# Gate sums scattered as sums and inverted on gathered rows, a count on GpSimd, and splits of expert 0's weights at other places

## The chip, the cores and the metric

The kernel runs on one core of a Trainium2 chip. The metric is device microseconds of one execution, start to end. The core's engines are TensorE (PE), VectorE (DVE), ScalarE (ACT) and GpSimd (POOL); SyncE (SP) issues the loads.

## What is computed

A linear attention with decay (4 batches, 8 heads, 768 tokens, head size 48), then a mixture of 8 experts in which each of the 3072 tokens goes to its best expert alone:

```python
for t in range(S):
    cur = np.einsum('bhd,bhe->bhde', u[None] * kt, vt)
    y[:, :, t] = np.einsum('bhd,bhde->bhe', rt, state + cur)
    state = wt[:, :, :, None] * state + np.einsum('bhd,bhe->bhde', kt, vt)
...
logits = x @ w_gate                       # x: 3072 x 384, w_gate: 384 x 8
expert_idx = np.argmax(logits, axis=1)
logits_shift = logits - logits.max(-1, keepdims=True)
probs = np.exp(logits_shift)
probs /= probs.sum(-1, keepdims=True) + 1e-09
gate_w = probs[np.arange(N), expert_idx]
for e in range(E):
    mask = expert_idx == e
    h = np.maximum(x[mask] @ w1[e], 0.0)  # w1[e]: 384 x 1024
    ye = h @ w2[e]                        # w2[e]: 1024 x 384
    out[mask] = gate_w[mask, None] * ye
```

The chosen expert's shifted logit is 0 and its exponential 1, so a token's weight is 1 over the sum of its 8 exponentials (and 1e-9).

## The kernel before

**The token loop.** Tokens are worked in blocks of 128 (a chunk) of one batch: NB = 24 blocks, 6 chunks of B = 4 batches. `iteration(n)` runs for n = -3 to 23 and holds work of several blocks at once. For a block, DVE runs two scans over decays (`suf` and `pre`), the products `kh` and `rh`, and `at`, which puts the masked products `ap` of PE beside the diagonal. POOL forms `rk` and clears triangles of `at` (L359); PE does the products; ACT copies diagonals (`at` L371), evicts (`ytb`, `xr`, `ls`) and scales states. `keep_warm` puts products of constants into PE's queue, whose result nobody reads: six in the coefficients of n = 0 and 1, two in some others.

**The gate.** GB = 8 blocks, a pair of chunks, go through the gate together (n = 9 and 17 for the first two pairs; the last pair goes in smaller groups). For each token DVE takes the maximum logit, the shifted logits `sh` and the one-hot `oh` of the choice. `count` adds the one-hots over the blocks (`ohs`) to the running `seen`; `place` works out each token's row in its expert's region, summing to `pf` and casting it to the integer `pi`; `act_ex` is the exponential `ex` on ACT, and `weigh` (n = 10 and 18) sums it (`se`), adds 1e-9 and writes the reciprocal into column DM of `xr`. A row of `xr` is a token's 384 values, then its weight (column DM), then its number. POOL scatters these rows to `xs` in memory by expert (an indirect DMA for each block). Rows that no token takes were filled before from `zrow`.

**The experts.** Products run in pairs of halves: each f32 weight is split into a high half (`w1h`, `w2h`, by ACT, L246) and a low one (`w1l`, `w2l`, by DVE, L248), the rows likewise (`x` and the second `x`, L301 and L302; hidden values `hh` L311 and `hl` L312), and three products stand for one. Expert 0's rows are worked in two parts of 192 and 236 rows: `pa` within the loop's end (`pa.trans`, `pa.mm1(0)` to `pa.mm1(7)`), `pb` behind it. `contract` is the second product of a part: 24 products into a bank `opt` for each half of the rows, evicted by `ort` on DVE (L325), which multiplies each row by its weight in column DM; POOL scatters `ort` to the output. Experts 1 to 7 follow in order of their token count, each with one load of rows (`load_x`, tile `xg`), a transposing split (`trans_x`), `mm1` and `mm2`.

**What sets the order.** Within the loop and the first expert the order on PE, DVE, ACT and POOL is written out by hand; behind it a scheduler sets it. SP's order is the order in which loads are written: the load of expert 1's rows stands behind the last token scatter and pb's rows, ahead of expert 1's remaining weights. Expert 0's weights are loaded early and are split in pieces of 128 x 512: twelve high halves, one for each n from 8 to 19, and the six w1 lows at n = 11, 12, 13, 14, 15 and 19, right behind `at`; the six w2 lows at n = 22 and 23 (two each, behind `at`) and two among `pa.mm1`.

## Time and profile before

| | |
|---|---|
| median of 3 runs | 408.28 us (407.12 to 409.44) |
| the profiled execution | 405.56 us |
| its span in the trace | 403.9 us |
| busy, share of the span: PE, DVE, ACT, POOL | 94%, 66%, 58%, 29% |
| instructions on PE, DVE, ACT, POOL | 3537, 493, 651, 162 |
| mean granted TensorE clock | 0.988 of full speed |

The span is what the trace covers; the profiled execution lasted 1.7 us more than it. The token loop takes the span's first 160 us or so, the experts the rest. Shares are means over both, so they are read by stretch. Line numbers L... are those of the kernel before; in the changed kernel the same lines stand 4 to 18 further down.

### The profile page before, as it was taken

To read this page: it belongs to the slowest core of one execution; us is meant where nothing else is said; L and a number is where in the kernel's file an instruction comes from. 1 tells how busy PE (TensorE), PEld (TensorE's weight loads), DVE (VectorE), ACT (ScalarE), POOL (GpSimd) and SP (SyncE) were. 2 spreads that over 40 slices of the span, in tenths; PEclk is the share of its full clock that TensorE was granted. 3 is DMA by queue.
4 is the path that set the end of the run, shared out by engine and by line. 5 is a ranking of instruction groups with operands and counts; after the bars stand their busy time and mean duration, and the time that the engine had idled before them with its cause. 6 is when DMAs were issued, how large, how long until landed. Compare 5 with 4: busy or idle time off the path is not lost.

```text
span 403.9 us, 9402 instructions
## 1 busy us (share of the span) xinstructions
PE 380.3 (94%) x3537; PEld 339.5 (84%) x3538; DVE 267.0 (66%) x493; ACT 234.0 (58%) x651; POOL 118.1 (29%) x162
## 2 busy tenths in 40 slices
PE   8898899898998889999999999999999999999994
PEld 6576677777776668989988999999999999999994
DVE  8799699999999997647774662562562672632321
ACT  8699799899999873236564543543552562420210
POOL 5543233495436946210300050040040050221001
PEclk9699999999999999999999999999999999999998
DMA  8999999999851223395789247246246244011001
GB/s 198 192 202 190 235 278 220 227 293 250 209 125 60 74 77 119 89 320 159 223 265 297 82 127 228 90 141 214 82 140 216 78 138 138 5 51 38 18 2 54
DMA packets 30159, 62.05 MB, mean 154 GB/s; under 512 B 4880, under 2 KB 17979, under 8 KB 30109
## 3 DMA queue, kind: packets, MB, share of 16 engines
q1 hardware_dynamic: 25500, 51.92, 48.7%
q0 software_dynamic: 4608, 9.48, 7.1%
q8 instruction: 29, 0.48, 0.5%
q14 instruction: 22, 0.17, 0.1%
HBM read 49.53 MB, written 12.20 MB: 153 GB/s over the span
## 4 chain that ended last, share of the span: by engine, by line
PE 65%; DVE 19%; ACT 6%; DMA 4%; issue 3%; POOL 1%; SPq 1%; POOLq 0%; ACTq 0%; DVEq 0%
PE bank L309 24%; PE bank L968 17%; PE opt L321 10%; DVE at L400 4%; DVE pre L393 4%; DVE suf L377 3%; PE ap L498 2%; PE pt L300 2%; DMA xg<-xs 2%; DVE kh L387 2%; PE op L957 2%; ACT at L371 2%; DMA rkwt<-in_rkw_dram 2%; PE lp L548 2%; PE kp L489 1%
## 5 line engine op out<-in xcount | busy, mean ns | idle before, releaser
L272 POOL DMA_INDIRECT out_dram<-ot,xg x26 | 30.1, 1159 | 169.3 <-DVE ot L958 126.8
L248 DVE TENSOR_TENSOR w2l<-wst,w2h 128x512 fp32r<-128x512 f32 x48 | 31.1, 682 | 42.5 <-ACT w2h L246 42.5
L309 PE MATMUL bank<-xl,w1h 128*128 128x384 f32 (+5 forms) x168 | 58.8, 353 | 0.0
L309 PE MATMUL bank<-xh,w1l 128*128 128x384 f32 (+5 forms) x168 | 58.4, 350 | 0.0
L309 PE MATMUL bank<-xh,w1h 128*128 128x384 f32 (+5 forms) x168 | 54.2, 355 | 0.0
L311 ACT ACTIVATE hh<-bank 128x384 fp32r<-128x384 f32 (+7 forms) x58 | 26.3, 470 | 39.0 <-PE bank L309 38.0
L371 ACT ACTIVATE at<-ident,ct 128x128 f32<-128x128 f32 x144 | 47.0, 395 | 0.0
L312 DVE SCALAR_TENSOR_TENSOR hl<-bank,hh 128x384 fp32r<-128x384 f32 (+7 forms) x58 | 29.8, 530 | 22.8 <-ACT hh L311 22.6
L344 POOL TENSOR_TENSOR rk<-rkwt 112x512 f32<-112x512 f32 x24 | 32.2, 1342 | 37.0 <-DVE pre L381 30.2
L498 PE MATMUL ap<-rh,kh 48*128 48x128 f32 (+1 forms) x384 | 29.2, 291 | 7.9 <-DVE rh L354 5.8
L248 DVE TENSOR_TENSOR w1l<-wst,w1h 128x512 fp32r<-128x512 f32 x48 | 31.4, 686 | 6.7 <-ACT w1h L246 6.0
L498 PEld LDWEIGHTS ap<-rh,kh 64*128 64x128 f32 (+1 forms) x384 | 24.3, 193 | 13.2 <-DVE rh L354 10.1
L246 ACT ACTIVATE w1h<-wst 128x512 fp32r<-128x512 f32 x48 | 28.5, 627 | 11.9 <-DMA wst<-in_w_dram 6.7
L400 DVE COPY_PREDICATED at<-cmask,ap 128x1024 f32<-128x1024 int32 x24 | 31.6, 1318 | 4.8 <-PE ap L498 4.4
L973 ACT ACTIVATE oT<-bank 128x464 f32<-128x464 f32 (+4 forms) x15 | 7.9, 523 | 46.2 <-PE bank L968 46.2
L968 PE MATMUL bank<-hh,w2l 128*128 128x408 f32 (+4 forms) x96 | 34.0, 356 | 0.0
L968 PE MATMUL bank<-hl,w2h 128*128 128x408 f32 (+4 forms) x96 | 33.9, 354 | 0.0
L968 PE MATMUL bank<-hh,w2h 128*128 128x408 f32 (+4 forms) x96 | 33.7, 356 | 0.0
L695 POOL DMA_INDIRECT xs<-xr,pi x24 | 28.8, 1198 | 16.6 <-DVE sh L569 5.4
L377 DVE TENSOR_TENSOR_SCAN suf<-rkwt,sufone 112x520 f32<-112x520 f32 x24 | 31.2, 1300 | 1.7 <-DMA rkwt<-in_rkw_dram 1.7
L309 PEld LDWEIGHTS bank<-xh,w1l 128*128 128x128 f32 x168 | 31.6, 188 | 0.8
L309 PEld LDWEIGHTS bank<-xl,w1h 128*128 128x128 f32 x168 | 31.4, 188 | 0.7
(169 smaller groups left out, 865.0 us busy)
## 6 DMA issues: line engine op xcount, KB each, us to landing
rkwt<-in_rkw_dram SPq DMA_DIRECT2D x44, 289.5 KB, 9.7
wst<-in_w_dram SPq DMA_DIRECT2D x48, 256.0 KB, 5.5
wst<-in_w_dram SPq DMA_DIRECT2D x16, 768.0 KB, 7.7
vt<-in_vv_dram SPq DMA_DIRECT2D x24, 192.0 KB, 9.0
xg<-xs SPq DMA_DIRECT2D x6, 579.0 KB, 5.4
xs<-zrow SPq DMA_DIRECT2D x8, 289.5 KB, 9.1
rkwt<-in_rkw_dram SPq DMA_DIRECT2D x4, 224.0 KB, 4.5
xg<-xs SPq DMA_DIRECT2D x1, 675.5 KB
```

The source lines that it names most:

```text
L248: nc.vector.tensor_tensor(out=lo, in0=st[:, cs], in1=hi.bitcast(F32), op=ALU.subtract)
L272: i = nc.gpsimd.indirect_dma_start(out=out[:, :], out_offset=bass.IndirectOffsetOnAxis(ap=t.bitcast(I32)[:, q, DM + 1:DM + 2], axis=0), in ...
L309: nc.tensor.matmul(hp, a, x[:, j, :], start=(i == 0), stop=(i == 8))
L312: nc.vector.scalar_tensor_tensor(out=hl, in0=hp, scalar=0.0, in1=hh.bitcast(F32), op0=ALU.max, op1=ALU.subtract)
L321: nc.tensor.matmul(op, a[:, cs], w2v(wt, w, f), start=(i == 0), stop=(i == 23))
L344: i = nc.gpsimd.tensor_tensor(out=d["rk"], in0=d["r"], in1=d["k"], op=ALU.mult)
L371: nc.scalar.activation(blk[n]["at"][:, j, q], ident, AF.Copy, scale=blk[n]["ct"][:, head(q, j):head(q, j) + 1])
L377: nc.vector.tensor_tensor_scan(out=suf[:, ::-1], data0=d["w"][:, ::-1], data1=sufone.rearrange("p q c -> p (q c)")[:, ::-1], initial=0.0, ...
L400: nc.vector.copy_predicated(out=d["at"].rearrange("p j q c -> p (j q) c"), mask=cmask.unsqueeze(1).broadcast_to([P, 2 * NP_, C]), data=d[" ...
L498: nc.tensor.matmul(d["ap"][:, j, q, :], d["kh"][rs, q, :], d["rh"][rs, q, :], start=True, stop=True)
L695: i = nc.gpsimd.indirect_dma_start(out=xsf, out_offset=bass.IndirectOffsetOnAxis(ap=ch["pi", c, b], axis=0), in_=xr[:, b, :], in_offset=No ...
L968: nc.tensor.matmul(pp, w, a, start=(i == 0), stop=(i == 23))
```

## The change

- `weigh` no longer inverts. The sums are written straight into column DM of `xr`; the 1e-9 is a ninth column of the two constant tiles `exs` that take turns for `ex`. The reciprocal is taken in place on the gathered rows: `pa.weights()`, `pb.weights()`, and at the head of `mm2` for experts 1 to 7. `zrow` gets 1.0 in column DM.
- `count` of a pair of chunks is four additions on GpSimd in place of a reduction and an addition on DVE.
- `place` sums straight to an integer; the cast is gone.
- The six high halves of w2 move from n = 14 to 19 to n = 22 and 23. The w1 lows of n = 14, 15 and 19 move to n = 22 (two) and 23 (one). All six w2 lows move behind `pa.mm1(7)`.
- `contract` does the 16 products with `w2h` first, then the 8 with `w2l`.
- `keep_warm` puts ten products at n = 1, not six.

```diff
     ebrow = const.tile([1, GB, E], BF16, name="ebrow")
     none = const.tile([1, 1], F32, name="none")
+    exs = [const.tile([P, GB, E + 1], F32, name=f"ex{i}") for i in range(2)]
     zrow = wst.tile([P, XC], F32, name="zrow", tag="wst")
...
         nc.gpsimd.memset(zrow, 0.0)
+        nc.gpsimd.memset(zrow[:, DM:DM + 1], 1.0)
...
+        for t in exs:
+            nc.gpsimd.memset(t[:, :, E:E + 1], 1e-9)
...
         op = xtile([rows, DM], "opt")
         i = 0
-        for f in range(8):
-            hh, hl = hs[f]
-            cs = slice(q * rows, (q + 1) * rows)
-            for a, w in ((hh, "h"), (hl, "h"), (hh, "l")):
-                nc.tensor.matmul(op, a[:, cs], w2v(wt, w, f), start=(i == 0), stop=(i == 23))
-                i += 1
+        cs = slice(q * rows, (q + 1) * rows)
+        for part in ("hl", "h"):
+            for f in range(8):
+                for x in part:
+                    nc.tensor.matmul(op, hs[f][x == "l"][:, cs], w2v(wt, "h" if part == "hl" else "l", f), start=(i == 0), stop=(i == 23))
+                    i += 1
...
-            keep_warm(t[:, C:], 6 if n < 2 else 2 if n < B or n - 3 in (2 * B, 4 * B) else 0)
+            keep_warm(t[:, C:], 10 if n == 1 else 6 if n < 2 else 2 if n < B or n - 3 in (2 * B, 4 * B) else 0)
...
     def act_ex(k):
-        ex = sm.tile([P, GB, E], F32, name="ex", tag="ex")[:, 0:k[2]]
-        nc.scalar.activation(ex, ch["r", k][0], AF.Exp)
+        ex = exs[nth["e"] % 2][:, 0:k[2]]
+        nth["e"] += 1
+        nc.scalar.activation(ex[:, :, 0:E], ch["r", k][0], AF.Exp)
...
         add = oh[:, 0, :]
-        if m > 1:
+        if m == GB:
+            part, w = oh, m // 2
+            while w:
+                half = sm.tile([P, w, E], F32, name="ohh", tag=f"ohh{w}", bufs=1)
+                nc.gpsimd.tensor_tensor(out=half, in0=part[:, 0:w], in1=part[:, w:2 * w], op=ALU.add)
+                part, w = half, w // 2
+            add = part[:, 0, :]
+        elif m > 1:
             add = sm.tile([P, E], F32, name="ohs", tag="ohs")
             nc.vector.tensor_reduce(out=add, in_=oh.rearrange("p b e -> p e b"), axis=AX.X, op=ALU.add)
-        nc.vector.tensor_tensor(out=new, in0=old, in1=add, op=ALU.add)
+        (nc.gpsimd if m == GB else nc.vector).tensor_tensor(out=new, in0=old, in1=add, op=ALU.add)
...
         c, b, m = k
-        se = sm.tile([P, GB], F32, name="se", tag="se")[:, 0:m]
-        nc.vector.tensor_reduce(out=se, in_=ch["ex", k], axis=AX.X, op=ALU.add)
-        nc.vector.tensor_scalar(out=se, in0=se, scalar1=1e-9, scalar2=None, op0=ALU.add)
         for i in range(0, m, B):
             w = min(B, m - i)
-            nc.vector.reciprocal(ch["xr", c + i // B][:, b:b + w, DM], se[:, i:i + w])
+            nc.vector.tensor_reduce(out=ch["xr", c + i // B][:, b:b + w, DM], in_=ch["ex", k][:, i:i + w], axis=AX.X, op=ALU.add)
...
-        pf = sm.tile([P, GB], F32, name="pf", tag="pf")[:, 0:m]
-        nc.vector.tensor_reduce(out=pf, in_=ps, axis=AX.X, op=ALU.add)
         pi = sm.tile([P, GB], I32, name="pi", tag="pi", bufs=3)[:, 0:m]
-        nc.vector.tensor_copy(pi, pf)
+        with nc.allow_low_precision("whole numbers below 2 ** 24"):
+            nc.vector.tensor_reduce(out=pi, in_=ps, axis=AX.X, op=ALU.add)
...
+        def weights(self):
+            nc.vector.reciprocal(self.t[:, :, DM:DM + 1], self.t[:, :, DM:DM + 1])
+
         def mm2(self, q):
             contract(wt0, self.hs, q, self.rows, self.t)
...
     lows = []
-    late = []
-
-    def late_lows(k):
-        for _ in range(k):
-            split_piece(*late.pop(0), half="l")
+    late = [(wt0, i, 3, p) for i in (2, 3) for p in range(3)]
+
+    def late_splits(half, ks):
+        for k in ks:
+            t, i, n, p = late[k]
+            split_piece(t, stg[0, i], i, n, p, half)
...
         dve_state(n - 1)
         dve_at(n)
-        if n in (11, 12, 13, 14, 15, 19):
+        if n in (11, 12, 13):
             split_piece(*lows.pop(0), half="l")
-        if n >= NB - 2:
-            late_lows(2)
+        for _ in range(2 if n == NB - 2 else 1 if n == NB - 1 else 0):
+            split_piece(*lows.pop(0), half="l")
         act_diag(n + 1, slice(0, 1) if n < 0 else slice(0, 3))
         if whole and b == 2:
             weigh(whole)
+        if n == NB - 2:
+            late_splits("h", range(0, 3))
...
             act_ex(pair)
+            late_splits("h", range(3, 6))
             place(pair)
...
-        m = n - 8
-        if 0 <= m < 12:
-            piece = (wt0, stg[0, m // 3], m // 3, 3, m % 3)
+        if 8 <= n < 14:
+            piece = (wt0, stg[0, (n - 8) // 3], (n - 8) // 3, 3, (n - 8) % 3)
             split_piece(*piece, half="h")
-            (lows if m < 6 else late).append(piece)
+            lows.append(piece)
...
         wt = wts[e % 2]
+        nc.vector.reciprocal(t[:, :, DM:DM + 1], t[:, :, DM:DM + 1])
...
         weigh(mid)
-        late_lows(1)
         pe_y(nl)
...
         count(end)
-        late_lows(1)
         pa.mm1(2)
...
         pa.mm1(7)
+        late_splits("l", range(6))
+        pa.weights()
         expert(1)
         pb = Part(HA, HB // 2)
         load_x(1)
...
         pb.trans()
         pa.mm2(1)
+        pb.weights()
         nth["b"] = 0
```

How this stands on the engines. First DVE from the last `hl` of `pa.mm1(7)` on, with `xg_2593` (before) and `xg_2589` (after) the gathered rows of `pa`, `xg_3026` those of `pb` and `xg` without a number those of expert 1 (`116x4`); before:

```order
L312 SCALAR_TENSOR_TENSOR hl<-bank,hh 128x192
L325 TENSOR_SCALAR ort<-opt,xg_2593 96x384
L302 TENSOR_TENSOR x_3047<-pt,x_3047 128x236 x3
L325 TENSOR_SCALAR ort<-opt,xg_2593 96x384
L312 SCALAR_TENSOR_TENSOR hhl<-bank,hhl 128x236 x2
L248 TENSOR_TENSOR w1l<-wst,w1h 128x512 x3
L312 SCALAR_TENSOR_TENSOR hl<-bank,hh 128x236 x3
L248 TENSOR_TENSOR w1l<-wst,w1h 128x512 x3
```

and after:

```order
L316 SCALAR_TENSOR_TENSOR hl<-bank,hh 128x192
L252 TENSOR_TENSOR w2l<-wst,w2h 128x512 x6
L733 RECIPROCAL xg_2589<-xg_2589 96x2
L953 RECIPROCAL xg<-xg 116x4
L329 TENSOR_SCALAR ort<-opt,xg_2589 96x384
L306 TENSOR_TENSOR x_3029<-pt,x_3029 128x236 x3
L329 TENSOR_SCALAR ort<-opt,xg_2589 96x384
L733 RECIPROCAL xg_3026<-xg_3026 118x2
L316 SCALAR_TENSOR_TENSOR hhl<-bank,hhl 128x236 x2
L252 TENSOR_TENSOR w1l<-wst,w1h 128x512 x3
L316 SCALAR_TENSOR_TENSOR hl<-bank,hh 128x236 x3
```

Six lows of w2 and two reciprocals stand between the last `hl` and the first `ort`, the second of them on expert 1's rows; that on pb's rows follows the second `ort`.

DVE at n = 9 and 10, from `place` to behind `weigh`; before:

```order
L632 TENSOR_TENSOR ps<-few,oh 128x64
L634 TENSOR_REDUCE pf<-ps 128x8
L636 CAST pi<-pf 128x8
L377 SCALAR_TENSOR_TENSOR suf<-rkwt,sufone 112x520
L381 RECIPROCAL pre_0_175<-suf 112x4
L408 TENSOR_TENSOR sst_190<-dp,gbd_189 112x192
L400 COPY_PREDICATED at<-cmask,ap 128x1024
L600 TENSOR_REDUCE se<-ex 128x8
L601 TENSOR_SCALAR se<-se 128x8
L604 RECIPROCAL xr<-se 128x4 x2
L387 TENSOR_TENSOR kh<-rkwt,suf 112x512
```

and after:

```order
L641 TENSOR_TENSOR ps<-few,oh 128x64
L644 TENSOR_REDUCE pi<-ps 128x8
L381 SCALAR_TENSOR_TENSOR suf<-rkwt,sufone 112x520
L385 RECIPROCAL pre_0_175<-suf 112x4
L412 TENSOR_TENSOR sst_190<-dp,gbd_189 112x192
L404 COPY_PREDICATED at<-cmask,ap 128x1024
L613 TENSOR_REDUCE xr<-ex_215 128x4 x2
L391 TENSOR_TENSOR kh<-rkwt,suf 112x512
```

Place is one instruction shorter; of the four of `weigh` two reductions are left.

POOL around the count of the first pair; before:

```order
L344 TENSOR_TENSOR rk<-rkwt 112x512
L359 AFFINE_SELECT at<-ct 128x256
L344 TENSOR_TENSOR rk<-rkwt 112x512
L359 AFFINE_SELECT at<-ct 128x256
L344 TENSOR_TENSOR rk<-rkwt 112x512
L607 IOTA xr 128x4
L359 AFFINE_SELECT at<-ct 128x256
L344 TENSOR_TENSOR rk<-rkwt 112x512
```

and after:

```order
L348 TENSOR_TENSOR rk<-rkwt 112x512
L363 AFFINE_SELECT at<-ct 128x256
L348 TENSOR_TENSOR rk<-rkwt 112x512
L363 AFFINE_SELECT at<-ct 128x256
L348 TENSOR_TENSOR rk<-rkwt 112x512
L599 TENSOR_TENSOR ohh<-oh 128x32
L599 TENSOR_TENSOR ohh<-ohh 128x16
L599 TENSOR_TENSOR ohh<-ohh 128x8
L605 TENSOR_TENSOR seen<-seen,ohh 128x8
L616 IOTA xr 128x4
L363 AFFINE_SELECT at<-ct 128x256
```

Four additions stand ahead of the row numbers (`IOTA xr`), where there were none.

## Rows read from the trace of the kernel before

**Rows 1.** Busy time by stretch (us, busy time with count per engine, PEclk, DMA share, GB/s).

```profile
67.00:99.00 32.00, 29.16 (x476) 22.54 (x474) 31.38 (x52) 29.57 (x100) 18.59 (x24) 1.00 1.01 254
118.00:138.00 20.00, 16.79 (x290) 13.22 (x293) 19.63 (x35) 18.21 (x63) 13.58 (x17) 1.00 0.15 53
168.00:400.00 232.00, 229.10 (x1319) 220.78 (x1317) 113.28 (x198) 93.03 (x188) 35.36 (x30) 1.00 0.44 137
```

**Rows 2.** Chain of waits in the token loop (start us, length us, engine and line).

```profile
70.79 0.17 DVE ohs L592
...
70.98 0.17 DVE seen L593
...
73.80 0.23 DVE pf L634
...
74.13 1.25 DVE suf L377
...
77.07 0.10 DVE se L600
...
77.20 0.18 DVE se L601
...
77.40 0.24 DVE xr L604 x2
...
100.82 0.57 DVE w1l L248
```

**Rows 3.** Timeline of Pool and DVE from 12.2 us (start, length, [idle before <- releaser]).

```profile
12.25 0.40 POOL L359 TENSOR_SCALAR_AFFINE_SELECT at<-ct 128x256 f32<-128x256 f32 x1
...
12.78 1.27 POOL L344 TENSOR_TENSOR rk<-rkwt 112x512 f32<-112x512 f32 x1
12.89 2.25 DVE L377 TENSOR_TENSOR_SCAN suf<-rkwt,sufone 112x520 f32<-112x520 f32 x1 [0.93 <-DMA rkwt<-in_rkw_dram]
```

**Rows 4.** Timeline of ACT in the last blocks.

```profile
149.21 0.27 ACT L551 ACTIVATE ls<-lp 64x128 f32<-64x128 f32 x1 [1.77 <-PE lp L548]
```

**Rows 5.** Groups by line: the high halves of a split (busy us, mean ns).

```profile
L246 ACT ACTIVATE w2h<-wst 128x512 fp32r<-128x512 f32 x48 | 27.8, 626 | 4.9 <-DMA wst<-in_w_dram 3.3 <-PE bank L968 1.4
```

**Rows 6.** Timeline of DVE around the first expert.

```profile
168.17 0.36 DVE L312 SCALAR_TENSOR_TENSOR hl<-bank,hh 128x192 fp32r<-128x192 f32 x1 [0.21 <-ACT hh L311]
171.99 0.61 DVE L325 TENSOR_SCALAR ort<-opt,xg 96x384 f32<-96x384 f32 x1 [3.47 <-PE opt L321]
...
180.78 1.90 DVE L248 TENSOR_TENSOR w1l<-wst,w1h 128x512 fp32r<-128x512 f32 x3 [0.28 <-ACT w1h L246]
```

**Rows 7.** Timeline of PE around the first expert.

```profile
172.66 0.42 PE L300 MATMUL pt<-ident,xg 118*128 118x118 f32 x2 [0.20 <-DVE ort L325]
173.16 0.42 PE L321 MATMUL opt<-w2h,hh 128*96 128x384 f32 x1
```

**Rows 8.** SP's waits, 165 to 180 us (us in total, times, longest).

```profile
SPq L235 <- DMA xg<-xs: 1.8, 1, 1.8
```

**Rows 9.** Timeline of SP's DMA issues, 165 to 180 us.

```profile
168.38 1.92 SPq L266 DMA_DIRECT2D xg<-xs  x4
...
175.59 0.38 SPq L235 DMA_DIRECT2D wst<-in_w_dram  x1
```

**Rows 10.** Timeline of PE and DVE at the start.

```profile
9.78 1.14 PE L143 MATMUL cp<-wz,ones 128*128 128x384 bf16 x6
...
12.35 0.66 PE L475 MATMUL cp<-rk,ubt 112*32 112x128 f32 x8 [1.43 <-POOL rk L344]
...
16.35 1.31 DVE L400 COPY_PREDICATED at<-cmask,ap 128x1024 f32<-128x1024 int32 x1 [0.99 <-PE ap L498]
```

**Rows 11.** Busy time and granted clock (PEclk) at the start.

```profile
5.35:12.18 6.83, 5.12 (x36) 2.49 (x34) 6.51 (x9) 5.23 (x11) 3.89 (x2) 1.00 1.06 223
12.18:19.00 6.82, 6.66 (x48) 4.47 (x49) 5.08 (x5) 4.66 (x17) 3.88 (x7) 0.50 1.05 182
```

More of the change, by code (lines that the diff above doesn't have):

```diff
@@ L87, in small @@
         return few["t"]
-    nth = {"b": 0, "h": 0, "x": 0}
+    nth = {"b": 0, "h": 0, "x": 0, "e": 0}
     def xtile(shape, name):
```

## Prediction

> **What bounds the kernel now.** The page's busy times, taken over the whole span, put PE first by far. That mean hides two kernels in one, so the first view to read is the busy time by stretch [rows 1]. From 168 us on, in the experts, PE is busy 229.10 of 232.00 us: there any microsecond in which PE stands is a microsecond of the result. In the token loop it is different. From 67 to 99 us DVE is busy 31.38 of 32.00 us, from 118 to 138 us 19.63 of 20.00, while PE has 29.16 and 16.79. Matching this, the chain of waits runs for long stretches from one DVE instruction into the next [rows 2]. So in the loop, work taken from DVE counts nearly in full, and after the loop only what stops or frees PE counts. The change does something to each side: it empties DVE in the loop, and it puts a wait in front of PE's work at about 172 us.
>
> **DVE work taken out of the loop.** I go by the chain's own pieces [rows 2].
> - Count of a pair (n = 9 and 17): ohs 0.17 and seen 0.17 with the 0.02 between them leave DVE: 0.36 each, 0.72 together.
> - Place (n = 9 and 17): from the start of pf (73.80) to that of suf (74.13) are 0.33. A reduce alone takes about 0.16 before the next one follows. Saved 0.17 each, 0.34 together.
> - Weigh (n = 10 and 18): from 77.07 to the end of xr are 0.57 for four instructions; two reduces of about the size of se (0.18 to 0.25 from start to start) stay. Saved about 0.22 each, 0.44 together.
> - Low halves w1l at n = 14, 15 and 19: 0.57 on the chain at 100.82, and two more pieces like it; 1.71 together.
>
> The sum is 3.21 us. The six w2h pieces leave ACT in n = 14 to 19 as well, so ACT does not take DVE's place as the bound in these blocks.
>
> **What that costs elsewhere.** Three w2h pieces come to stand before `ls` of n = 22 and three behind `ex` of n = 23. ACT waits there for PE anyway, 1.77 us before the `ls` of n = 22 [rows 4] and longer before the next, and three pieces of 0.63, as splits on ACT take [rows 5], need 1.9: nothing, or 0.1. The three w1l lows go to n = 22 and 23 and replace four w2l lows there: nothing. The count goes to Pool as four small instructions. Pool's price is bounded by its 0.40 for a 128x256 select and its 1.27 for a 112x512 product [rows 3]; four operands of 128x32 and less should take 0.2 each. Pool's own time is free at n = 9. But two engines can hold each other up: a suf that started 0.11 behind Pool's rk took 2.25 [rows 3], against 1.25 in the loop [rows 2], so it waited about as long as rk ran. A DVE instruction that meets one of the four small ones then loses up to 0.2 to 0.4. I take 0.2 per pair, at least 0 and at most 0.5. The loop's gain is thus 2.8 us, between 2.2 and 3.2.
>
> On this the Trainium skill ("SBUF — State Buffer", section "Who interferes with whom") says that a DVE instruction with two SBUF inputs and a GpSimd instruction that reads SBUF exclude each other for the whole instruction, whichever began first. The 2.25 agrees. If each of the four met such a DVE instruction, the rule would make it 0.8 per pair instead of 0.2, and the gain 1.6.
>
> **The reciprocals, and the wait that they bring.** The sums' reciprocals are now taken on the gathered rows, nine small instructions of about 0.2 us. Eight of them find their rows landed long before or sit where DVE idles. One does not. On DVE, behind the last `hl` of the first part, the new order is: six w2l lows, the reciprocal of part one's rows, **the reciprocal of expert 1's rows**, and only then `ort`, which evicts the first `opt`. Expert 1's rows are loaded late: SP issues that load with the last two of the four issues that fill 168.38 to 170.30 [rows 9], behind the last token scatter. The first thing that shows its landing is SP's wait for it before a weight load, 1.8 us long [rows 8], after which that load is issued at 175.59 [rows 9]. So the rows land at about 175.45; the small second piece of the same load, issued last, may land up to 0.7 later.
>
> Until now nothing needed these rows before PE transposes them, after both parts of the first expert are done. Now `ort` does, and behind it on DVE are the second half of pb's split (`x` minus) and the second `ort`. Who waits for that: PE. In the trace, PE stood 0.20 us on the first `ort` and began the second `opt` at 173.16 [rows 7], with `ort` running 171.99 to 172.60 [rows 6]. In the new order:
> - The six lows begin when `hl` ends (168.53) [rows 6] and take 3.8, since three such took 1.90 [rows 6]: done at 172.3. As `contract` now takes all high products first, PE meets the lows late, and the first `opt` ends some 0.5 us later than it did.
> - The last scatter begins 0.6 to 0.8 earlier relative to PE, since one cast, one TENSOR_SCALAR, one reciprocal and a low no longer stand before it; so the rows are there at 174.7 to 175.4, against PE's old time.
> - Reciprocal 0.2, `ort` 0.61, the two last transposes 0.42: the second `opt` begins between 175.9 and 177.0, not at 173.16.
>
> PE loses 3.3 us (2.6 to 3.9). A little could be won back at later short waits of PE; with PE busy 229.10 of 232.00 us [rows 1] I take nothing for it. Uncovered, this wait alone is larger than the loop's gain. SP's queue is not reordered, and Pool's scatters of `ort` have time.
>
> **The start.** Between 5.35 and 12.18 us the granted clock was 1.00 and between 12.18 and 19.00 it was 0.50 [rows 11], the lower of TensorE's two levels, 1.2 against 2.4 GHz. What came before was an idle gap of PE of 1.43 us, until Pool's rk was done, ending at 12.35 [rows 10]. Six dummy products took 1.14 [rows 10]; ten fill about 0.7 of this gap. If the clock then holds, DVE's idle 0.99 before the first `at` [rows 10] goes, and in the blocks behind it the chain runs over PE too: 0.5 to 1.6, I take 1.1. If it doesn't, the four dummies lie in a gap and cost nothing. I see no reason in the trace for one or the other: one half each.
>
> **The sum.** -2.8 (loop) + 3.3 (wait) + 0 (ACT, SP) gives +0.5 with the old start, and -0.6 with a start at full clock. The profiled execution took 405.56 us, 403.9 of them the span, 2.7 less than the median 408.28; the difference is added to the median. That is 408.8 or 407.7; I say 408.2. No measurable change, then, 0.5% (2.0 us) being about what a measurement of this kernel can tell from none.
>
> **The rivals.**
> 1. *The wait is followed by half clock* (slower). PE idle for 3.3 us in one piece is more than all of PE's idle time from 168 to 400 us, 2.90 [rows 1], and the one stretch at half clock, 6.82 us long [rows 11], followed a gap of less than half that. If PE's idle time at 173 to 176 brings such a stretch, the products behind it take twice their time: 3.4 us lost, with PE as the bound. Then 408.2 + 3.4 = 411.6 (410 to 412.5). It decides from the point at which the gap is long enough to make the clock fall; the trace has only the one case to go by. The Trainium skill ("TensorE: Matmul & The Clock Gate", section "Why this matters for your kernels") warns that an idle gap between bursts of products puts the engine back on its low clock; it speaks for this rival, and this case's one fall agrees.
> 2. *The wait isn't there* (faster). Either the load lands earlier than SP's wait tells, or the wait on the second piece falls where DVE has nothing else. For it: the landing is known from another engine's wait alone. Against: SP's queue stood 1.8 us for it, until just before 175.59 [rows 8, 9]. Then -2.8, with either start: 404.4 to 405.5.
> 3. *Pool eats the gain.* In n = 18 to 21 two token scatters per block stand in Pool's queue, and if Pool sets the pace once DVE has less, what n = 18 and 19 gave (0.22 and 0.57) is lost, and with locks at the upper bound another 0.6: 1.4 of the 2.8, 409.6. Against it: from 118 to 138 us Pool is busy 13.58 of 20.00 us [rows 1].
>
> **How the numbers follow.** Forecast, the wait with the clock kept: 0.45 (406.7 to 409.5). Rival 1: 0.31. Rival 2: 0.16. Rival 3: 0.08, on the border of measurable. Faster by over 0.5% is rival 2 and the edge of the forecast (a load that lands early, and a full-clock start): 0.18. Slower is rival 1 and part of rival 3: 0.35. The rest, 0.47, is within 0.5%. The range leaves out the faster half of rival 2 and the upper edge of rival 1: 404.7 to 411.9.
>
> **What would show it.** DVE's list at 170 to 177 must show `ort` idle before it, ended by the DMA of xg, and PE a gap of about 3 us before the second `opt`; the granted clock of the 7 us behind that gap decides rival 1. The last `hl` of the first part, at 168.17 before [rows 6], should start 2.8 us earlier, or 3.9 with the start's gain; the granted clock of 12 to 19 us tells the start. If DVE's chain is broken by waits for Pool in n = 18 to 21, rival 3 holds. The forecast is wrong if PE's gap is under 1 us, or if the loop gives less than 2.

## The result and the profile after

| | before | changed | ratio (95%) |
|---|---|---|---|
| median of 4 runs each | 407.77 us (407.12 to 409.44) | 413.33 us (412.83 to 414.86) | 1.0136 [1.0093, 1.018] |
| the profiled execution | 405.56 us | 412.84 us | |
| its span | 403.9 us | 411.1 us | |
| its mean granted clock | 0.988 | 0.972 | |

Slower by 1.4%, and outside the range of 404.7 to 411.9. But the two sides did not run at the same clock: the four changed runs had mean granted clocks of 0.964 to 0.976, the one run of before whose clock is listed 0.988. The same file was therefore timed twice more, on two chips (experiments 5 and 9): 1.0011 [0.9977, 1.0045] and 1.0013 [0.9968, 1.0059], at clocks of 0.975 to 0.996. In experiment 9 two more runs, at 0.963 and 0.962, took 414.33 and 414.96 us, which is where the four changed runs above lie. So there are two questions: what the change itself does, which is close to nothing in sum, and where the first measurement's 5.6 us came from. (The ratios leave out runs more than 1.5% above the fastest of the same measurement, so the four changed runs, all alike, stay in; the profiles of experiments 4, 11 and 12 were taken in such runs, and no time after their first 60 us is compared.)

The page of the changed kernel: busy times, and the granted clock in 40 slices of the span (9 is full).

```profile
PE 386.0 (94%) x3541; PEld 344.5 (84%) x3542; DVE 265.8 (65%) x480; ACT 234.0 (57%) x651; POOL 123.3 (30%) x173
...
PEclk9999999999999759969999999999999999999998
```

The dents stand in slices 14, 15 and 18, not at the start. The busy times by stretch tell them apart (columns as in [rows 1]: busy time per engine, then granted clock, DMA share, GB/s):

```profile
5.35:12.18 6.83, 6.38 (x49) 3.33 (x48) 6.76 (x8) 5.23 (x11) 4.57 (x3) 1.00 1.05 237
12.18:19.00 6.82, 5.49 (x72) 4.01 (x72) 6.72 (x8) 6.79 (x25) 4.29 (x7) 1.00 1.08 206
135.06:141.89 6.83, 4.80 (x55) 3.51 (x53) 5.10 (x11) 4.94 (x19) 3.53 (x8) 0.78 0.32 99
141.89:148.72 6.83, 6.46 (x62) 5.03 (x62) 3.01 (x7) 4.63 (x15) 0.30 (x1) 0.50 0.08 28
148.72:155.54 6.82, 6.74 (x69) 5.45 (x68) 2.70 (x14) 3.85 (x11) 4.28 (x8) 0.72 0.31 116
...
176.46:183.28 6.82, 5.96 (x20) 5.28 (x21) 1.74 (x5) 0.37 (x1) 0.94 (x1) 0.50 0.84 305
```

The start, at half clock before [rows 11], is now at full clock. In its place there are two other stretches at 0.50: 13.65 us at the loop's end (138.91 to 152.56) and 6.82 us from 176.46. The second lies exactly where the prediction looked. DVE's timeline around the first expert (start, length, idle before and its releaser), then PE's:

```profile
169.44 0.36 DVE L316 SCALAR_TENSOR_TENSOR hl<-bank,hh 128x192 fp32r<-128x192 f32 x1
169.72 3.69 DVE L252 TENSOR_TENSOR w2l<-wst,w2h 128x512 fp32r<-128x512 f32 x6
...
176.55 0.18 DVE L953 RECIPROCAL xg<-xg 116x4 f32<-116x4 f32 x1 [3.07 <-DMA xg<-xs]
176.65 0.61 DVE L329 TENSOR_SCALAR ort<-opt,xg 96x384 f32<-96x384 f32 x1
```

```profile
173.46 0.59 PE L325 MATMUL opt<-w2l,hh 128*96 128x384 f32 x2 [0.19 <-DVE w2l L252]
173.90 0.57 PE L304 MATMUL pt<-ident,xg 118*128 118x118 f32 x4
177.32 0.66 PE L304 MATMUL pt<-ident,xg 118*128 118x118 f32 x2 [2.86 <-DVE ort L329]
177.64 0.65 PE L325 MATMUL opt<-w2h,hh 128*96 128x384 f32 x1
178.09 0.53 PE L325 MATMUL opt<-w2h,hl 128*96 128x384 f32 x1
```

DVE, in order, stands 3.07 us on expert 1's rows with `ort` behind it; PE stands 2.86 us on `ort` [rows 7: 0.20 before]; and the products behind it start 0.32 to 0.45 us apart, where those of the first `opt` in the same profile started 0.17 to 0.18 apart.

The span split at the same instructions, changed minus before in us; 'same clock' is the profile of experiment 5, the same file, whose only half-rate stretch, apart from the last microseconds, is 3.41 us long:

| stretch | changed | same clock |
|---|---|---|
| start to `at` of n = 5 | -3.3 | -2.2 |
| to `at` of n = 21 | -2.8 | -3.6 |
| to the first `opt` product (loop's end) | +7.4 | +0.2 |
| to the first `ort` | +3.4 | +3.7 |
| to the third `ort` (behind the wait) | +2.4 | +0.9 |
| to the end | +0.2 | +1.3 |
| sum | +7.3 | +0.3 |

(The last stretch took 212.8 to 214.5 us in the profiles of all kernels but those three, 213.15 in that of before, in no order with the edits.)

### The profile page after: what moved, and what is told of

It is laid out like the page before. It is cut to its first block, busy times and chain, and to the rows that moved or that the text cites. A ratio compares the mean times of both kernels' runs of the same rounds, so it can differ in the third digit from the quotient of the medians.

```text
span 411.1 us, 9418 instructions
## 1 busy us (share of the span) xinstructions
PE 386.0 (94%) x3541; PEld 344.5 (84%) x3542; DVE 265.8 (65%) x480; ACT 234.0 (57%) x651; POOL 123.3 (30%) x173
## 4 chain that ended last, share of the span: by engine, by line
PE 64%; DMA 11%; DVE 10%; ACT 6%; POOL 4%; issue 3%; SPq 1%; POOLq 0%; ACTq 0%; DVEq 0%
PE bank L313 24%; PE bank L983 17%; PE opt L325 9%; DMA xg<-xs 3%; DMA rkwt<-in_rkw_dram 3%; PE ap L502 2%; PE pt L304 2%; DVE at L404 2%; DMA xs<-zrow 2%; DMA vt<-in_vv_dram 2%; DVE pre L397 2%; DVE suf L381 2%; PE yp L538 2%; PE op L972 2%; POOL xs L703 2%
## 5 line engine op out<-in xcount | busy, mean ns | idle before, releaser
L502 PE MATMUL ap<-rh,kh 64*128 64x128 f32 (+1 forms) x384 | 29.3, 294 | 8.3 <-DVE rh L358 7.0
L703 POOL DMA_INDIRECT xs<-xr,pi x24 | 29.8, 1241 | 19.9 <-DVE mx L571 7.2
L250 ACT ACTIVATE w2h<-wst 128x512 fp32r<-128x512 f32 x48 | 27.3, 625 | 7.5 <-DMA wst<-in_w_dram 6.0
```

The lines of the kernel that those rows point to most:

```text
L250: nc.scalar.activation(hi, st[:, cs], AF.Copy)
L502: nc.tensor.matmul(d["ap"][:, j, q, :], d["kh"][rs, q, :], d["rh"][rs, q, :], start=True, stop=True)
L703: i = nc.gpsimd.indirect_dma_start(out=xsf, out_offset=bass.IndirectOffsetOnAxis(ap=ch["pi", c, b], axis=0), in_=xr[:, b, :], in_offset=No ...
```

## The experiments

My theory after the result: the wait costs about what was predicted, the clock falls behind it each time, and the loop-end fall is either the change's own doing (PE idles more once DVE is quicker) or chance. The rival: the moved splits hold up the loop's end. 'Changed' below is the kernel after the change.

| | edit | ratio to before (95%) |
|---|---|---|
| 1, 10 | expert 1's reciprocal late | 0.9898 [0.9823, 0.9972]; 0.994 [0.9897, 0.9983] |
| 2 | dummies in the loop's end | 0.9991 [0.9929, 1.0054] |
| 3 | both of these | 0.9939 [0.9856, 1.0022] |
| 4 | before, ten dummies | 0.9916 [0.9836, 0.9997] |
| 5, 9 | changed, again | 1.0011 [0.9977, 1.0045]; 1.0013 [0.9968, 1.0059] |
| 6, 11 | 1, splits at their old places | 0.9917 [0.9883, 0.9951]; 0.9987 [0.9943, 1.0032] |
| 7 | before, with the wait alone | 1.0102 [1.0069, 1.0134] |
| 8 | changed, wait filled with dummies | 1.0043 [1.0003, 1.0083] |
| 12 | 1, w2's lows spread | 0.9937 [0.9887, 0.9986] |

Experiments 1 to 4, 5 to 8 and 9 to 12 ran on three different chips.

**1. The wait taken away.** Expert 1's reciprocal moves behind `pb.mm2(1)`, where its rows have long landed.

```diff
-        nc.vector.reciprocal(t[:, :, DM:DM + 1], t[:, :, DM:DM + 1])
+        if e > NST:
+            nc.vector.reciprocal(t[:, :, DM:DM + 1], t[:, :, DM:DM + 1])
...
         pb.mm2(1)
+        nc.vector.reciprocal(xg[1][:, :, DM:DM + 1], xg[1][:, :, DM:DM + 1])
```

> The changed kernel, but the reciprocal of expert 1's rows is taken behind the second part's last eviction, when the rows have long landed, instead of ahead of the first eviction of the first part. Theory: PE's stand of 2.86 us at 174.5 (row of the changed kernel's trace, ended by ort) goes, and with it the half-rate stretch from 176.46 to 183.28, which costs half of 6.8 us: 413.3 - 2.9 - 3.4 = 407.0, and the granted clock stays 1.00 from 160 us on. Rival, the second fall of the clock has another cause (it came 37.5 us after the first): only 2.9 goes, 410.4, with a half-rate stretch in the experts.

Faster than before. DVE's `ort` now waits only for PE, and the clock behind it stays up:

```profile
169.56 0.61 DVE L329 TENSOR_SCALAR ort<-opt,xg 96x384 f32<-96x384 f32 x1 [0.61 <-PE opt L325]
```

```profile
138.28:141.70 3.42, 3.42 (x31) 3.02 (x32) 1.11 (x6) 2.78 (x12) 0.41 (x1) 0.50 0.38 109
168.00:176.00 8.00, 7.34 (x44) 6.14 (x44) 3.36 (x9) 0.99 (x3) 0.94 (x1) 1.00 0.99 324
```

From the first `opt` product to the first `ort` it takes 5.22 us, 4.38 before and 7.77 in the changed kernel. The 0.84 that stay are the six lows in a row, which PE meets late. The loop's end has a fall here too, but of 3.42 us, not 13.65, and up to 169 us the two programs are the same.

**2. Dummies in the loop's end.** Four dummy products ahead of `ap` for n = 18 to 21 and six in the coefficients of n = 22 and 23; the reciprocal stays early.

```diff
+            keep_warm(t[:, C:], 6 if n in (22, 23) else 0)
...
+            if 18 <= n < 22:
+                keep_warm(d["ap"][:, 0, 0:3, :].rearrange("p q c -> p (q c)"), 4)
```

> The changed kernel with products of constants put into PE's queue, results unread: four ahead of ap at n = 18 to 21 and six behind the coefficients at n = 20 and 21. Theory: the half-rate stretch from 138.91 to 152.56 follows PE's gaps there (1.37 at 128.82, 1.66 at 139.16); filled, the clock holds, and the gain of 6.1 us that at shows at n = 21 (135.53 against 141.61) reaches the first expert: 413.3 less about 6.8 = 406.5. Rival, the loss between n = 21 and the first expert comes from the moved splits on ACT and DVE or from Pool's scatters and not from the clock: the dummies add up to 2 us of PE work in the last blocks, 413 to 415.

The clock held from 139 to 153 us, but the dummies stood ahead of `ap` in PE's queue: `at` of n = 21 came at 138.61, against 134.66 in experiment 1 on the same chip, and at n = 23 it was still 1.7 behind (151.96 against 150.26). They cost more than they saved. The fall behind the wait was there (174.53 to 177.95).

**3. Both.** The edits of 1 and 2 together.

```diff
+        if e > NST:
...
+            keep_warm(t[:, C:], 6 if n in (22, 23) else 0)
...
+                keep_warm(d["ap"][:, 0, 0:3, :].rearrange("p q c -> p (q c)"), 4)
```

> Both edits: the reciprocal of expert 1's rows late, and the dummy products at n = 18 to 21. Theory: both losses go, 413.3 - 6.3 - 6.8 = 400.2, with the granted clock at 1.00 throughout. Rival, moved splits and Pool set the end of the loop: about 407, as with the late reciprocal alone.

No stretch at half clock before the tail, and yet not distinguishable from 1 or from before. Even so `at` of n = 23 began 8.2 us after that of n = 22 (5.9 before), DVE idle 2.51 ahead of it: something other than the clock delays the loop's end here (see the last section).

**4. Before with ten dummies at n = 1.**

```diff
-            keep_warm(t[:, C:], 6 if n < 2 else 2 if n < B or n - 3 in (2 * B, 4 * B) else 0)
+            keep_warm(t[:, C:], 10 if n == 1 else 6 if n < 2 else 2 if n < B or n - 3 in (2 * B, 4 * B) else 0)
```

> The kernel before with ten dummy products in place of six in the coefficients of n = 1, nothing else. Theory: the changed kernel's early gain is the start's: its at was 1.30 us earlier at n = 0 and 3.31 at n = 8, before any other edit acts, and the clock was 1.00 between 12 and 19 us instead of 0.50. So 407.8 - 3.3 = 404.5 if the clock then holds to the end. Rival, the start's clock depends on where the run's phase falls and not on the dummies: 0.50 between 12 and 19 us again, 407.8.

`at` of n = 5 begins 2.9 us earlier than in the profile of before, at full clock. By itself this would give the start's gain to the dummies; experiment 7 takes it back. The ratio, 0.9916, has its interval just below 1, from three runs, and was not measured again.

**5. The changed kernel again, on another chip.** No edit.

> The changed kernel as it is, on the chip of the runs beside it. Up to 169 us it is the same program as the one with the late reciprocal, which had its clock at half for 3.4 us in the loop (138.28 to 141.70) where the changed kernel had 13.65 (138.91 to 152.56). Theory: the length of that stretch varies from chip or run, and the changed kernel is here about 6.3 above the late reciprocal's 404.9 (2.9 of waiting, 3.4 of half clock behind it): 411. Rival: the loop's long half-rate stretch belongs to the changed kernel in every run: 413, as at first.

404.63 against 404.54 us. Profile: windows as above, of the loop's end and of the 3.41 us behind the wait; then DVE.

```profile
135.06:141.89 6.83, 5.83 (x94) 4.46 (x91) 6.18 (x12) 6.83 (x27) 4.00 (x8) 1.00 0.33 107
141.89:148.72 6.83, 6.46 (x94) 5.31 (x92) 6.25 (x22) 5.64 (x16) 3.32 (x7) 1.00 0.23 85
170.67:174.08 3.41, 3.38 (x12) 2.97 (x13) 1.00 (x3) 0.37 (x1) 0.94 (x1) 0.50 1.06 383
```

```profile
140.92 1.32 DVE L404 COPY_PREDICATED at<-cmask,ap 128x1024 f32<-128x1024 int32 x1 [0.42 <-PE ap L502]
...
146.80 1.32 DVE L404 COPY_PREDICATED at<-cmask,ap 128x1024 f32<-128x1024 int32 x1 [0.25 <-PE ap L502]
...
169.95 0.18 DVE L953 RECIPROCAL xg<-xg 116x4 f32<-116x4 f32 x1 [3.42 <-DMA xg<-xs]
```

The loop's end is whole, the wait is there, and so is the fall behind it. The first measurement's loss at the loop's end is thus no fixed property of the changed program.

**6. Experiment 1 with the splits at their old places** (w2's highs at n = 14 to 19, its lows at n = 22, 23 and behind the loop, w1's lows at n = 14, 15 and 19), so that of the loop's edits only gate, place and count remain.

```diff
-        if n in (11, 12, 13):
-            split_piece(*lows.pop(0), half="l")
-        for _ in range(2 if n == NB - 2 else 1 if n == NB - 1 else 0):
+        if n in (11, 12, 13, 14, 15, 19):
             split_piece(*lows.pop(0), half="l")
+        if n >= NB - 2:
+            late_lows(2)
...
-        if n == NB - 2:
-            late_splits("h", range(0, 3))
...
-        late_splits("l", range(6))
```

> The kernel with the late reciprocal, but every split (w2h, w1l, w2l) where the kernel before has it; the gate's, count's and start's edits stay. Theory (moved splits are the larger half of the loop's gain, 1.71 of 3.21): at of n = 19 comes 1.7 to 2.2 us later than with the moved splits (124.11), and the total is about 1.5 above 404.9, 406.4. Rival: what the moved splits gain in n = 14 to 19 is given back at n = 22 and 23, where at of n = 23 came 8.1 us after that of n = 22 (5.89 before): then the total is the same or better, 403.5 to 405.

From `at` of n = 8 to that of n = 23 it takes 88.28 us, 90.13 before, 86.49 in experiment 5 and 86.48 in 8. So gate, place and count give 1.8 and the moved splits another 1.8. Behind `hl` the first `ort` follows as before, 4.40 us from the first `opt` product: the 0.84 of experiment 1 is the lows' place indeed.

```profile
166.66 0.61 DVE L329 TENSOR_SCALAR ort<-opt,xg 96x384 f32<-96x384 f32 x1 [3.41 <-PE opt L325]
```

**7. Before, with the wait alone.** A copy of four columns of expert 1's rows on DVE ahead of `pa.mm2(0)`.

```diff
+        seen1 = ld.tile([P, 4], F32, name="seen1", tag="vt")
+        nc.vector.tensor_copy(seen1[0:xg[1].shape[0], :], xg[1][:, :, DM])
         pa.mm2(0)
```

> The kernel before with one small DVE copy that reads expert 1's rows ahead of the first eviction of the first part, so that only the wait is added. Theory: DVE idles until the load lands, 175.5 to 176.1, PE stands 3.3 to 3.9 us before the second opt, and a half-rate stretch of 6.8 us follows: 408.5 + 3.5 + 3.4 = 415. Rival, the wait costs its own length but not the clock: 412.

Slower, 408.24 against 404.54 us: the wait as such, with its fall, costs about 1%. These 3.7 us are near the rival's 3.5 and half of the 6.9 expected, although the fall is there. The profile has 3.9 us lost up to the first `ort` and 2.1 behind it, 6.0 in all; where the medians make up the rest is not shown. Windows of this kernel, then DVE and PE:

```profile
5.35:12.18 6.83, 5.94 (x46) 3.09 (x44) 6.73 (x8) 5.87 (x14) 4.93 (x3) 1.00 1.05 243
12.18:19.00 6.82, 4.77 (x69) 3.49 (x68) 6.75 (x8) 6.78 (x24) 3.95 (x6) 1.00 1.05 223
171.83:178.66 6.83, 5.75 (x19) 5.11 (x20) 1.72 (x5) 0.37 (x1) 0.94 (x1) 0.50 0.84 307
```

```profile
172.15 0.17 DVE L1036 COPY seen<-xg 116x4 f32<-116x4 f32 x1 [7.25 <-DMA xg<-xs]
172.24 0.61 DVE L325 TENSOR_SCALAR ort<-opt,xg 96x384 f32<-96x384 f32 x1
```

```profile
172.91 0.66 PE L300 MATMUL pt<-ident,xg 118*128 118x118 f32 x2 [4.17 <-DVE ort L325]
173.23 0.65 PE L321 MATMUL opt<-w2h,hh 128*96 128x384 f32 x1
173.68 0.53 PE L321 MATMUL opt<-w2h,hl 128*96 128x384 f32 x1
```

It also has the old six dummies at n = 1, and its start is at full clock all the same: `at` of n = 5 at 43.08, 46.68 in the profile of before and 43.1 to 44.4 in all the others. Behind the six dummies PE stood 0.39 us, 1.43 in the profile of before [rows 10]:

```profile
11.04 0.42 PE L475 MATMUL cp<-rk,ubt 112*32 112x128 f32 x8 [0.39 <-POOL rk L344]
```

**8. The wait filled.** Eighteen dummy products on PE between `pa.mm2(0)` and `pb.trans()`.

```diff
         pa.mm2(0)
+        keep_warm(bank(384), 18)
         pb.trans()
```

> The changed kernel with 18 dummy products (about 2.9 us) in PE's queue between the first opt and the transposes of the second part, so that PE works while it waits for expert 1's rows. Theory: the wait keeps its length (2.9, at most 0.4 more), but the clock stays at 1.00 behind it and 3.4 us come back: 3.0 to 3.4 below the changed kernel beside it. Rival: the fall at 176.46 doesn't come from the idle gap; same time as the changed kernel.

The one profile with the wait in which the clock did not fall behind it:

```profile
166.06 3.10 PE L143 MATMUL bank<-wz,ones 128*128 128x384 bf16 x18
168.99 0.77 PE L304 MATMUL pt<-ident,xg 118*128 118x118 f32 x6
170.25 0.42 PE L325 MATMUL opt<-w2h,hh 128*96 128x384 f32 x1 [0.49 <-DVE x L306]
```

```profile
168.45:175.28 6.83, 6.34 (x42) 5.58 (x40) 2.12 (x7) 0.89 (x3) 0.94 (x1) 1.00 0.75 272
```

DVE still waited for the rows, 2.67 us. So it is PE's idleness, not the wait of DVE, that brings the fall. The total says nothing for it: 406.04 us, where 3.0 to 3.4 below experiment 5 was expected and it is not below it, with clocks of 0.983 to 0.998 over its ten runs. Whether the filling pays is not settled.

**9. The changed kernel on a third chip**, and **10. experiment 1 on the same.** No edits beyond those above.

> The changed kernel a third time, beside the late reciprocal with the same program up to 169 us. Theory: the distance to the kernel before goes by how long the clock stands at half, which no edit here sets: with clocks of 0.98 to 0.995, as on the second chip, the same as before (within 2 us); with 0.96 to 0.975, as at first, 4 to 6 us slower. Rival: the 0.1 us of the second chip was the exception, and it is 4 to 6 us slower whatever its clock.

> The late reciprocal with all other edits, on the chip of the changed kernel. Theory: the wait alone costs 3.7 to 4.0 us (the first eviction came 8.1 to 8.3 us behind the first product of opt, against 4.4 before and 5.2 here) and up to 3.4 with the clock: 4 to 6 us below the changed kernel, and 3 to 4 below the kernel before. Rival: 3 us below the changed kernel at most, since PE has other waits that close up.

The late reciprocal repeats as faster, the changed kernel as equal to before. Between the two lie 2.1 us (medians of the runs in the ratios, 405.34 and 407.46), not the 4 to 6 expected: the rival's "3 us at most" holds. In 9 the fall behind the wait is there again (171.54 to 174.96). In 10 the stretch in which the first profile ran at half clock is whole; the programs are the same up to 169 us:

```profile
138.91:152.56 13.65, 11.03 (x157) 8.58 (x149) 9.15 (x29) 10.89 (x35) 6.34 (x14) 1.00 0.27 91
```

That profile took 2.5 us longer than that of 9 from `at` of n = 5 to that of n = 21 (93.83 against 91.31), also at full clock: the clock is not all that differs between runs of one program.

**11. Experiment 6 on the third chip** (the same edit), and **12. experiment 1 with w2's lows in pairs** behind `pa.mm1(5)`, `(6)` and `(7)`:

```diff
+        late_splits("l", range(0, 2))
...
+        late_splits("l", range(2, 4))
...
-        late_splits("l", range(6))
+        late_splits("l", range(4, 6))
```

> The late reciprocal with the splits where the kernel before has them, beside the one with moved splits. Theory: the moved splits give 1.8 in the loop (at of n = 23 is 88.3 behind that of n = 8 with the splits back, 86.5 with them moved) and cost 0.8 before the first eviction: the moved ones are 1.0 us faster. Rival: they gain nothing in all; same time within 0.5 us, or the splits back faster.

> The late reciprocal and the moved splits, with the six w2 lows in pairs behind the sixth, seventh and eighth block of the first part's first product, not all six behind the eighth. Theory: DVE idles between these blocks; the first eviction comes 4.4 us behind the first opt, not 5.2, and the total is 0.6 to 0.8 below the kernel with six in a row. Rival: the lows delay the sorting of the experts or hl on DVE, and the load of the experts' rows with it: the same or slower.

Experiment 6's advantage did not repeat, and 12 is no better than 10 at this resolution; whether its first `ort` came earlier is not shown, its profile being one of the three. Which split places are best beside the late reciprocal stays open. On the third chip the kernels with an interval below 1 are 10 and 12, by about 0.6%; only the late reciprocal with the moved splits was below 1 in both of its measurements (1 and 10).

## Why the prediction was wrong

**Taken from the loop: right in mechanism, undersized.** Predicted 2.8 us (2.2 to 3.2), measured 3.6 from n = 8 to n = 23 (experiments 5 and 8). The splits gave 1.8, as priced (1.71). Gate, place and count gave 1.8, not 1.1. One term that was mis-sized is the 0.2 per pair for Pool and DVE holding each other up. From `at` of n = 9 to that of n = 10, with count and place in between, it took 6.29 us before and 5.76 in experiment 5:

```profile
69.46 1.33 DVE L400 COPY_PREDICATED at<-cmask,ap 128x1024 f32<-128x1024 int32 x1
...
75.75 1.32 DVE L400 COPY_PREDICATED at<-cmask,ap 128x1024 f32<-128x1024 int32 x1
```

```profile
67.21 1.31 DVE L404 COPY_PREDICATED at<-cmask,ap 128x1024 f32<-128x1024 int32 x1
...
72.97 1.32 DVE L404 COPY_PREDICATED at<-cmask,ap 128x1024 f32<-128x1024 int32 x1
```

These 0.53 are all of the 0.36 and 0.17 forecast for the two, with nothing lost; from n = 17 to 18 it was 0.48. Pool's count in experiment 5, and DVE's timeline beside it and at `weigh`:

```profile
68.37 0.25 POOL L599 TENSOR_TENSOR ohh<-oh 128x32 f32<-128x32 bf16 x1
68.69 1.65 POOL L599 TENSOR_TENSOR ohh<-ohh 128x16 f32<-128x16 f32 x2
```

```profile
68.43 0.74 DVE L391 TENSOR_TENSOR kh<-rkwt,suf 112x512 f32<-112x512 f32 x1
69.09 1.26 DVE L397 TENSOR_TENSOR_SCAN pre<-rkwt,pre 112x520 f32<-112x520 f32 x1
...
71.24 0.22 DVE L644 TENSOR_REDUCE pi<-ps 128x8 int32<-128x64 f32 x1
...
74.19 0.27 DVE L613 TENSOR_REDUCE xr<-ex 128x4 f32<-128x36 f32 x2
74.39 0.68 DVE L391 TENSOR_TENSOR kh<-rkwt,suf 112x512 f32<-112x512 f32 x1
74.98 1.24 DVE L397 TENSOR_TENSOR_SCAN pre<-rkwt,pre 112x520 f32<-112x520 f32 x1
```

Two additions of Pool took 1.65 together while `kh` and `pre` ran, where the larger one ahead of them took 0.25; `kh` and `pre` took 0.74 and 1.26, against 0.68 and 1.24 one block on. Here Pool paid, and Pool had time. The Trainium skill ("SBUF — State Buffer", section "Who interferes with whom") has the one of the two that began first hold the other off; the rows fit that, with Pool the one held off. Nothing in the sum rests on this. The other term is `weigh`: two reductions take 0.20 to 0.27 where the four instructions took 0.57 [rows 2], and from `at` of n = 10 to that of n = 11 it took 0.37 us less than before, from n = 18 to 19 0.50 less, where 0.22 was taken.

**Costs on ACT: right.** With the clock up, the loop's end costs 0.2 more than before (26.19 us from `at` of n = 21 to the first `opt` product in experiments 5 and 8, 26.00 before).

**The start: right in the clock, wrong in the cause and the size.** I gave one half to a full-clock start through the four dummies. Experiment 7 has six and the same start. The half clock of [rows 11] thus doesn't belong to the kernel before; its profile was 2.2 to 3.6 us long by it, where 1.1 was taken. With the six dummies the gap behind them was 1.43 us in one profile and 0.39 in the other, so whether that gap brought the half clock, as rival 1 had it, cannot be told from these runs, nor what the dummies themselves do.

**The wait: right.** `ort` waits for xg's DMA, PE stands 2.86 us, and from the first `opt` product to the first `ort` 3.4 to 3.7 us are lost (changed, 5 and 9: 7.77, 8.11, 7.79 against 4.38), of it 0.84 for the lows. Predicted 3.3 (2.6 to 3.9). DVE saw the landing up to 0.5 later than SP, as the second piece's bound of 0.7 allowed (experiment 5: SP issues on at 169.57, DVE starts at 169.95). Rival 2 falls.

**The clock behind the wait: the first step that failed.** The forecast, 0.45, was that the clock is kept; rival 1 had 0.31. The clock fell in all five profiles in which PE idled there (changed, 2, 5, 7, 9), and in none of the five without that gap (1, 3, 6, 10, and 8, where dummies filled it). Rival 1 should have been the likeliest. Its size, by the time from the first to the third `ort` against 18.72 before, was 0.9 us (5, 9) and 1.7 (2) where the stretch was 3.4 us long, and 2.1 to 2.4 where it was 6.8 (7, changed); I took 3.4 throughout, the loss of a PE at half rate for all of 6.8 us. The Trainium skill ("TensorE: Matmul & The Clock Gate", section "Why this matters for your kernels") warned of such an idle gap between bursts of products, and the five falls agree, behind gaps of 2.32 to 4.17 us.

**The clock at the loop's end: the second step, and the one that put the time outside.** The prediction knew two places at which the clock could differ. The third, 13.65 us at half clock, lies in the largest single item of the first profile: +7.4 us up to the first `opt` product. (In the profiles of experiments 9 and 10, at full clock there, that stretch is 2.6 us longer than in 5 and 8 for another reason, told in the last section; the changed profile has that too, 2.1 us at n = 23, so some 4.7 us are left to the clock.) There PE has gaps while DVE sets the pace, and a half-rate PE then becomes the one that DVE waits for:

```profile
135.53 1.32 DVE L404 COPY_PREDICATED at<-cmask,ap 128x1024 f32<-128x1024 int32 x1
...
143.76 1.31 DVE L404 COPY_PREDICATED at<-cmask,ap 128x1024 f32<-128x1024 int32 x1 [2.60 <-PE ap L502]
...
155.32 1.32 DVE L404 COPY_PREDICATED at<-cmask,ap 128x1024 f32<-128x1024 int32 x1 [2.91 <-PE few L631]
```

The same program up to there had 13.65, 3.42 and no us at half clock there in the profiles of changed, 1 and 10, and none in 5, 8 and 9. So it is not fixed by the edit. Nor do the runs show that the change makes it likelier: side by side on the same chips, every run counted, 3 of 22 of the changed kernel (experiments 5 and 9) and 9 of 55 of before have a mean clock of 0.976 or below. And in the profile of experiment 4, whose loop is that of before but for the dummies at n = 1, the clock stood at 0.50 for 6.83 us from 127.94 and for 17.07 us from 158.66. Why all four runs of the first measurement had a low clock stays open. By straight lines through the runs in the ratios (24 of changed, 52 of before on the three later chips), 0.01 of clock goes with 3.6 us (changed) and 2.6 us (before). With one slope for both, 3.1 us, an estimate from all these runs, changed and before come to 403.3 and 403.2 us at full clock.

**Rival 3 falls.** From 59 to 136 us DVE waited for Pool once, 0.8 us, in the changed profile, and in experiment 5 not in any wait that the trace lists.

So the sum -2.8 + 3.3, 'no measurable change', is what was measured in two of the three measurements of the changed kernel, in part by luck, since each piece is larger and the errors cancel: -3.6 in the loop, +3.4 to 3.7 for the wait and the lows, +0.9 or more for the clock behind it. What it lacked was a range for the clock of the run as a whole. The median of before, to which the prediction added its sum, carries its own share of half-rate time, and the changed kernel drew another share. The chance of slower was too small; a range up to some 415 would have held it.

## What to carry to other kernels

- When an instruction is moved forward on an in-order engine, look up when its data land: a 0.2 us reciprocal put ahead of an eviction cost 2.6 to 2.9 us here (3.4 to 3.7 less the 0.84 of the lows), and putting it where its rows have landed kept the loop's gain and made the kernel 1.0% and 0.6% faster than before (experiments 1 and 10).
- A new gap on PE like those here, 2.3 to 4.2 us, is to be priced with the half-rate stretch behind it, 0.9 to 2.4 us here, and not as a lesser possibility.
- Before a difference between two medians is put down to an edit, set the runs' mean granted clocks side by side: here 0.01 of clock went with 2.6 to 3.6 us, about as much as the largest part of the change, and the half-rate stretches sat now at the start, now at the loop's end, now behind the wait.

## What the runs showed of the hardware

- **The clock's falls do not repeat in place.** Programs that are the same up to 169 us ran 13.65, 3.42 and 0 us of the loop's end at 0.50 (changed, experiments 1 and 10). The Trainium skill ("TensorE: Matmul & The Clock Gate", section "What's actually happening") says of a kernel's start that the number of slow products varies from run to run; these profiles show the same in mid-kernel.
- **Products that end late for their reader.** In the profiles of experiments 1, 2, 3, 9 and 10 DVE's `at` of n = 23 began 2.3 to 2.4 us after the recorded end of the `ap` that it reads, at full clock. In experiment 1:

```profile
146.73 1.16 PE L502 MATMUL ap<-rh,kh 64*128 64x128 f32 x16
...
149.21 1.32 PE L552 MATMUL lp<-ytb,wgt 112*32 112x128 f32 x8
```

```profile
150.26 1.29 DVE L404 COPY_PREDICATED at<-cmask,ap 128x1024 f32<-128x1024 int32 x1 [2.50 <-PE few L631]
```

  `ap` ends at 147.89 and `at` begins at 150.26. In experiment 10 it is 150.02 and 152.37. The four profiles of experiments 5 to 8, on one chip, and that of before don't show it: 0.1 us. It makes the loop's end some 2.5 us longer (28.8 us in experiments 9 and 10 against 26.2 in 5 and 8). Whether the product ends later than the record models, or something else holds `at`, was not found; nor whether the kernel before has it on those chips, since no profile of that file was taken there.
- **A reduction of f32 into an integer** took 0.22 us (`pi` at 71.24 in experiment 5), against 0.23 for `pf` before [rows 2]: writing integers cost nothing, and the cast's time was saved whole.
